# The decay multiplies of a gated linear attention split between VectorE and GpSimd, with all steps laid out anew

## The chip, the cores and the metric

One core of a Trainium2 chip runs the whole program. Its engines are TensorE (PE; its weight loads are shown apart as PEld), VectorE (DVE), ScalarE (ACT), GpSimd (POOL) and SyncE (SP), which here issues all transfers. The metric is the device time of one execution in microseconds. Three runs of the kernel before gave 840.4, 843.08 and 843.6 us; the median is 843.08.

## What is computed

A gated linear attention over 4 batches, 8 heads, 768 tokens and 48 dimensions, with a complex decay for each token and dimension, and a two-layer MLP behind it:

```python
mag = np.sqrt(a_re * a_re + a_im * a_im)
scale = np.minimum(mag, 0.999) / (mag + 1e-06)
a_re_n, a_im_n = (a_re * scale, a_im * scale)
for t in range(S):
    ar, ai = (a_re_n[:, :, t, :, None], a_im_n[:, :, t, :, None])
    new_re = ar * S_re - ai * S_im
    new_im = ar * S_im + ai * S_re
    kv = np.einsum('bhd,bhe->bhde', k[:, :, t], v[:, :, t])
    S_re, S_im = (new_re + kv, new_im)
    y[:, :, t] = np.einsum('bhd,bhde->bhe', q[:, :, t], S_re)
...
x = np.ascontiguousarray(attn_out.transpose(0, 2, 1, 3)).reshape(B * S, H * D)
h = x @ w_in                                           # 384 -> 2048
g = np.maximum(h, 0.0) + alpha * np.minimum(h, 0.0)
return (g @ w_out).astype(np.float32)                  # 2048 -> 384
```

All of it is in float32; the weights arrive as 64-bit floats and are turned into float32 on the chip.

## The kernel before

The sequence is cut into 24 units of 128 tokens (4 batches of 6). The recurrence inside a unit isn't run token by token: a unit's queries and keys are multiplied by products of decays level by level, with block lengths h = 1, 2, 4, 8, 16, 32. At level h each block of 2h tokens has a left and a right half; keys of the left half meet queries of the right half in small TensorE products (`ps_lv`, L678), these are masked into the tiles `A` (L699 on ACT, L702 on DVE), and all of them multiply the values (`ps_y`, L817). Then the level's halves are multiplied with their decays, so that the next level can use them. What a unit leaves to later ones goes through the state `St` (L826, L829, and `ps_kv`, L797), and its part of the output through L841; L855 copies the output out, and it goes to DRAM and comes back as `xT` for the MLP.

`KQ` holds a unit's queries and keys: 96 partitions (48 dimensions, real and imaginary), and on each partition queries or keys x 8 heads x 128 tokens. `T` holds the tree of decay products. L661 and L663 turn queries and keys by their phases `PP`. The six levels are done in three visits of two levels, `VISITS = [(1, 2), (4, 8), (16, 32)]`. In each visit ACT copies the operands that TensorE needs gathered (`WQ`, L740: queries and keys of a level; `W`, L756: keys alone), DVE does the first level's multiply, then TensorE does both levels' products (`meet`), then DVE does the second level's multiply. That multiply is `step` (L717): one DVE operation on 1024 elements of each of the 96 partitions, 512 of queries (right halves) and 512 of keys (left halves). The transposed keys (`ps_kt`, L785) come behind the last level.

The decay products themselves (`gates`) are computed for half a batch at a time: ACT and DVE do the large operations (L253 to L318, L338, L426, L429), POOL the small ones for all batches but the first (L318 to L411: chains of small multiplies that depend on each other). POOL also does one step of the weights' conversion (L515, 16 times); DVE does the steps behind it (L517, L519).

The MLP runs for groups of one or two units as soon as their `xT` is there: 672 products for the hidden features (`ps_h`, L889, three for each of 16 feature blocks), ACT and DVE evict them through the activation (L896, L898) into `g_sb`, and 384 products give the output (`ps_o`, L908). Two `ps_h` buffers and one `ps_o` buffer are used in turn.

What sets the order: every part of the work is a Python generator that yields before each operation, and `ORDER` is a long string in which each letter says which generator goes on next (A to I the nine gate groups, J the loads of queries, keys, phases and decays, K and L the values, M pieces of the weights, N and O their conversion, P to m the 24 units, n the loads of `xT`, o the MLP). The arguments of a `yield` (an engine, a size, what it waits for) are not used at run time here: `DVE = ACT = POOL = PE = DMA = step` with a `step` that returns nothing. So each engine's instruction stream is fixed by the string, each engine runs its stream in order, and semaphores hold an instruction until its inputs are written and its buffers are free. `KQ` has three buffers, `T` two, `WQ` two, `W` one, `PP` one.

Of the kernel before, what the change touches and what calls it, by code (L numbers as in the profile page):

```python
# [14 lines left out]
ALU = mybir.AluOpType  # L15
# [15 lines left out]
    "AAAAAAAAAAAAAAAABJJJJBBAAAAAAAAMMMMMAMAAAAAAAAAAALLLBBNNBBLABLAAALABALAAAANBNABBBBANAABABBANABOOAMBB"  # L31
    "OBBOAAAAAAKMAABBBABABABABABBAKKKKAALLKAABABABAABAABNAAAAABANBABALAAABAABNBNOBBBBOOOOBONBMNBNNBBBBNNJ"
    "OBOOOOOBBPBPCBNPCBBBBPCBBBBCCJJJOBBOBBKPPPPBCBBBBBMPNJJLNNBPNNBPBPBPBCNPBNCMBMCPPPPPJPCKKKKKKKKKKKKK"
    "BKBKPBBBMBCPBNOCNBOOBPCMNCLLCCBLPPPPPPPPPPPPPPPPCCMCBCCBKCCCPJOCOCDOJOCNNJCNNNNNCDCCKKKPCPCPPPPPPPPP"
    "CCQCOKOOOCMQCCQLDDDQCCLLLLLLJLLLLLLCLCCCJDJJJJJJJCCNJQQCDNCQCQCDDQQCDCCNNQCDDQQDDQCOCODDCDCDCCCQDDOQ"
    "CQOCQQQCDDDDKOCRQQCRQQQQQQCQQQRRRRQQQQQMnQCNDMCOCOOCDDDMCQCLQCLRCCCCRCRRLLLRCRRRoKJLQOOOOCoRoCoCRRCR"
    "oQQLLLLLoooKLLQLoQQQoQCoCDCooRooQoRRDooCCCCRRRRRRRRRRoCRCoCoCoCDoRQCJJJEooRRODooooNNNNNoEDRooRoRoooo"
    "RDnLLLLooOoOoOoRODLooRoLLLLLLRLLDNRNoLSoooooooooSoRRRRRooJJSooOoooooSoSSDSNDSSSESoooooooRoSNSSoooSDo"
    "ooSSSDJSJJEJJJJJJDoooooDoooEOSSSSooooSDoooSSSSSSooDDDDDDDooETTSSSEESooooSSSSSToSSEEESSooKSSSoSToJTTT"
    "ToooToooSToooTooSLoooToULoDLLoLDTJDDDDDDJTDoToEDTDDoDLDLoDDDDDDooLLLLLoToTLTooooooooooToTTTUTTToTooT"  # L40
    "ooTLJooDTTToooDUUTTTTTToULLLLULEEEEooEoTEoEDDDDDDDDDoDDEooooooUEToooUUUoooooonoUoEooJoUoooooUEUEDTDD"
    "DoTTUUUELEJULoooLLKLLLLKoUoooooDDooDDDJoKDKKoKoooUUUUUUooooDDDTTTTTToUoooUDUUUooooUooDUEDUUUUEUEEEoo"
    "EoEoooooooEoEEUooUooJooEoooUUUUoUUoFUUoooEEEoEoEooooooooooEEoEoEVFooFoJVVooJoFoJJnooooJJJJVJVFoLLooo"
    "oooooVVVFFLoLVoooooooooEEEEEEVoooVVVEEEEEEEEEEELEEEoEJJJooFoWWoEEoEEEVooooVVooVoooWJVVVVFLoooWooLooo"
    "oWVVVVVVWVWWJVoooVFFVooooXVWLoLLLVLLoLooKVKoEEEEWEVVVVVVVVVVVKLLWEEVoKooLLLLLooLXFWLVLLVLVLVVWWWWWoE"
    "EEEELooWooooEoEoEWEEEooJEWWWWWWWWEoooooooooJJEoEJEEEoooEWWWooooWoooWWWWWWWWWXLoooooWoFFFLXoLLXXXoXXo"
    "GLLWWooJoJLLXooXoXWWWWWWooooFoFFXXXXXXFoLooooLooFoXoFoFFFFFFFJJooFooonXoXXXXXGLLLLooFFXooooooXXXXooo"
    "XoXoFYFFFooooFoooFooXoFXXXXXXXXXFFXXXXXJJoYYJoooooLJLJFFFGoooFYLGFFFFFFFFooXoooYYYYYJYoYooXoooooooLo"
    "FFFFFoZZYYYYJooJYoYYZooooooYoooooZGoYYYYYYYYoYFLZZZZZZZFooooLoYYLFFLGFLLLLFLLooooYYoZZoYYYJYYYYJJLJJ"
    "LLGoFZZZLLFLLFLLLLFLooooLFFFFFFFFFFFooZZYooFFFFYZoGGGGFoooFYYYYYYYYZZZoooFooLooooFFFFFFZJFFFZooZZZZZ"  # L50
    "FZFoooooJZooZoZZnZZZZooZZZZZJZaZZLLFFJoLooooZZZJoooFoGaooGooaoaooooGGGLLLLLLLoLLLaaaaoooooooooaJaJaJ"
    "ooooooaGaaaaaoooHoooHoaaooooooGGoooaaGaaaGGaaaGGGooGGGooboaaaKboooooJooooooaooooaHGbGaGJGbJoaaGaabbb"
    "bJoJaaaaaabaaGLLbLLLoGoLGoLLLGaaHooHJooobboGoooooobboooGHobbbHobbooooJbooGHoJoboLHGJoooGbbbGbGbbbbJb"
    "ooocooooGoooJoonbooKoKGccoKKKKKooooooLbcccGcccooooHoooocooGoLLLbGJoJobbbobHbHGHHbbbLbHbGbbbbbLbbboGG"
    "GGGHoHoHoLoooGGGGGoGcGLcoGoGooGGGoGoGoGcGcGcccccLJoJoLooLoooLooooLLLcccLLccLdocoJocGcoGcGccGoocodooc"
    "oHHHddcHcccccccHdLcGGcGKoooLLHHGGHLoHLJLLHHoHooHooHooHdcGcdcdddcHcccooodoooGoooGGGGoGLLdLLLLLoGGGodd"
    "dddoooododoooonooooGooGodGddddooGdoddoooooooGHGddHoodJodHHHoJoJJJHHHJJJooooodooooooddddddddddddddddo"
    "HJeeooooJooooeoooooeoHooHHHHHHHdoLeeeooooooeeeeoefoofoooeeeoeoeooooJJooofLoooooLLooIeeofffeJeeooKooo"
    "oLLLLLLLLLHeeeeeeeeHHHHLooHoHoHoHeHoHeHooeeeeeeeeeeeeeeeJJIJJLLoHHeeHooHHIHfKHHfHHHHHoooHoJHoHooHffJ"
    "ooHoofgIooogoooofffILoHHoofffHoofofHHogHooooLnooooLLLooLoJoLgLHKLffffffffggoLIILggggfoooofKooooKHooL"  # L60
    "HooHgHooooHoHKKoKKHoofoIfKooofffoffffffffffLfJoJoofHfffHoooooHggggggoLLLLLooooIogoogIoooooHggIIIIooo"
    "ooooLgoggLgLLLILoooogggggoooIgILoooogggggggggggggJJJoohJJhhoLLIIJoooJJoggLgoooJooohhILLLoIoInoooLoho"
    "oiiJJhJohoLLJLLLhooooIIooooooooohhohhoIooooooihIhhhoIhhhoIIoIoIhIIIooiooooooooIIIihihhhhhhhooohLILIo"
    "oIooooIohooJJhJooohohoohhhhhIIIiIhIhhLhhhhLLoLooooiiiiooLoooLooooiiiooihohihhihooioioooooooJijJjiiJJ"
    "JIIIIIIIIIIIIIIIIIIIIIIIIIIooiooooIojooiooioioioooooiooooIIijIIIoIIoojjjjjILoIiiIoILoLILoLoLLLiijiij"
    "ioiLLLLLLLjjjLLLiLLoooIIIIIoooiooIIIIIiooooooooooooooijjjojojooLLoooooooojjjjijjjjIIiiiiooojoojooiii"
    "jjjIooJjjjjjjjjjjjjnjoJJJjjjjooooooooooooookooookokokooLoooLJJJJJJJooooooLookkooookkokokookookooookk"
    "kkkkkLLLooooooLLLLLLLoooookkkkoookkkkokooLookookkllokokkJkkkkkkkkkkkkkkololooooooooLLoooLooookLooLLL"
    "LllllllllLoLoooooooooJooooooooooooooooooooooonooooooooooooooooooJoooLLLollloooooooolllloooJooooooJJl"
    "loooooJLlllllllllooooooooololoolllllllllllllllllooooooomooooLoooomoooooooooomooooommmmmmomooooomoooo"  # L70
    "ooooLmmLmLLoooonooLomooooooooomLmmmLooooLLommmmmmmmoooooooomomomLLooooooooooomoooooooLomommmmmmmmmmm"
    "mmmomooooooooooooooooooooooooooooooooooooooooooooooooooooooooooooooooonooooooooooooooooooooooooooooo"
    "oooooooooooooooooooooooooooooooooooooooooooooooooooooooooooooooooooooooooooooooooooooooooooo")
# [28 lines left out]
def kernel(  # L102
# [542 lines left out]
    def unit(u):  # L645
# [62 lines left out]
        def step(h, x0=None):  # L708

            at = TL - TL // h if h > 1 else 0  # L710
            if h > 1:
                x, m = ([(2 * h, H * P // (2 * h)), (H * P - h, 2), (1, h)], [(TL, H), (1, P // h), (0, h)])
            else:
                x, m = ([(H * P - 1, 2), (P, H), (2, HC)], [(1, 2), (TL, H), (2, HC)])
            x = bass.AP(tensor=KQ.tensor, offset=KQ.offset + h, ap=[KQ.ap[0]] + x)
            m = bass.AP(tensor=T.tensor, offset=T.offset + at, ap=[[T.ap[0][0], D2]] + m)
            nc.vector.tensor_tensor(out=x, in0=x if x0 is None else x0, in1=m, op=ALU.mult)  # L717

        if c == 0:
# [4 lines left out]
            k_ = yield DVE(H * D, k_, ("start", 0))  # L724
            nc.vector.tensor_tensor(out=St, in0=St, in1=start[:, b].unsqueeze(2).to_broadcast([D2, H, D]), op=ALU.mult)
            state[b] = (St, k_)
        k_ = r
        for visit in VISITS:
            ready = []
            for h in visit:  # L730
# [270 lines left out]
```

## Time and profile before

| What | Value |
| --- | --- |
| median of three runs | 843.08 us |
| the profiled execution | span 845.2 us |
| PE busy | 699.6 us (83% of the span) |
| DVE busy | 653.3 us (77%), 1020 instructions |
| ACT busy | 443.3 us (52%) |
| POOL busy | 196.3 us (23%), 293 instructions |
| DMA queue q1 | 129.20 MB, 59.2% of 16 engines |
| L717, the decay multiplies | 144 on DVE, 178.7 us busy |
| feature and output products, L889 and L908 | 302.0 and 295.2 us busy |

The span is cut into 40 equal slices; each digit is the busy share of an engine in tenths:

```profile
PE   0002316688899999999999999999999999999998
DVE  5999998689998999979998997687877656345212
ACT  7679686356745656665565634555444324233211
POOL 6241421126544411450115404300124000000000
```

Busy time counts from an instruction's start to its end, also where it stands still in between because of something else. Neighbouring instructions of one engine overlap by some 0.08 us. The chain that ended last (each step followed back to what released it) is 63% PE and 17% DVE.

### The profile page before, as it was taken

The page shows a single profiled execution, that of the slowest core. Times are in us where ns is not written, and L with a number is a line of the kernel's source. Part 1 is how long each engine was busy: PE and PEld are TensorE (multiplying, and loading weights), DVE is VectorE, ACT ScalarE, POOL GpSimd, SP SyncE. Part 2 cuts the span into 40 slices and gives each one's busy share as a digit, 9 for nine tenths or more (in the row PEclk, how much of TensorE's full clock was granted, in tenths as well). Part 3 has the DMA queues.
Part 4 walks back from the last instruction along what each step waited for, and adds up shares of the span by engine and source line. Part 5 has one row for each costly group of instructions (what it writes and reads, how often), then busy time and mean ns, then how long its engine had stood idle before and what let it go on. Part 6 is the DMA issues. An engine that isn't in the chain of part 4 may idle for free.

```text
span 845.2 us, 26866 instructions
## 1 busy us (share of the span) xinstructions
PE 699.6 (83%) x11488; PEld 529.6 (63%) x11488; DVE 653.3 (77%) x1020; ACT 443.3 (52%) x937; POOL 196.3 (23%) x293
## 2 busy tenths in 40 slices
PE   0002316688899999999999999999999999999998
PEld 0001315566777777767777777777676777777776
DVE  5999998689998999979998997687877656345212
ACT  7679686356745656665565634555444324233211
POOL 6241421126544411450115404300124000000000
PEclk9999997879999999999999999999999999999999
DMA  8496987675469677736965467747644482231100
GB/s 240 142 270 172 281 198 207 186 203 123 118 201 255 143 182 223 182 88 172 264 166 138 134 178 181 201 107 192 159 136 106 115 204 64 69 80 38 37 29 9
DMA packets 194174, 130.91 MB, mean 155 GB/s; under 512 B 74120, under 2 KB 185864, under 8 KB 194056
## 3 DMA queue, kind: packets, MB, share of 16 engines
q1 hardware_dynamic: 194056, 129.20, 59.2%
q8 instruction: 90, 1.47, 0.8%
q14 instruction: 28, 0.23, 0.1%
HBM read 100.82 MB, written 35.71 MB: 162 GB/s over the span
## 4 chain that ended last, share of the span: by engine, by line
PE 63%; DVE 17%; DMA 6%; issue 6%; ACT 5%; SPq 2%; POOL 0%; DVEq 0%; ACTq 0%; POOLq 0%
PE ps_o L908 25%; PE ps_h L889 25%; PE ps_lv L678 4%; DVE KQ L717 4%; PE ps_y L817 3%; PE ps_kv L797 2%; PE ps_y L841 2%; DVE gate L338 2%; DMA PP<-phs 2%; DMA phs<-gate 1%; DMA g_sb<-in_w_in_dram 1%; PE ps_kt L785 1%; DVE gate L426 1%; SPq L626 1%; DVE gate L340 1%
## 5 line engine op out<-in xcount | busy, mean ns | idle before, releaser
L889 PE MATMUL ps_h<-xT,w_in_sb 128*128 128x256 f32 (+1 forms) x1344 | 302.0, 356 | 2.9 <-DVE g_sb L898 1.6
L908 PE MATMUL ps_o<-w_out_sb,g_sb 128*128 128x384 f32 x768 | 295.2, 499 | 5.1 <-DVE g_sb L898 4.9
L889 PEld LDWEIGHTS ps_h<-xT,w_in_sb 128*128 128x128 f32 x1344 | 234.3, 193 | 74.1 <-issue 3.6
L898 DVE SCALAR_TENSOR_TENSOR g_sb<-g_sb,al,ps_h 128x256 f32<-128x256 f32 (+1 forms) x224 | 97.4, 437 | 115.5 <-ACT g_sb L896 115.1
L896 ACT ACTIVATE g_sb<-ps_h 128x256 f32<-128x256 f32 (+1 forms) x224 | 79.0, 353 | 204.2 <-PE ps_h L889 202.7
L908 PEld LDWEIGHTS ps_o<-w_out_sb,g_sb 128*128 128x128 f32 x768 | 138.0, 192 | 56.7 <-DVE g_sb L898 6.9
L717 DVE TENSOR_TENSOR KQ<-KQ,T 96x1024 f32<-96x1024 f32 x120 | 148.5, 1239 | 32.1 <-PE ps_lv L678 23.2
L678 PE MATMUL ps_lv<-WQ 96*32 96x32 f32 x2304 | 34.7, 204 | 79.0 <-DVE WQ L661 55.9
L678 PEld LDWEIGHTS ps_lv<-WQ 96*32 96x32 f32 x2304 | 26.6, 116 | 99.7 <-DVE WQ L661 56.1
L740 ACT COPY WQ<-KQ 96x1024 f32<-96x1024 f32 x48 | 50.0, 1041 | 27.8 <-DVE KQ L717 27.7
L338 POOL TENSOR_TENSOR gate<-gate 128x72 f32<-128x72 f32 x42 | 29.6, 704 | 125.6 <-ACT gate L368 122.8
L855 ACT COPY T<-ps_y 48x256 f32<-48x256 f32 x96 | 30.8, 364 | 51.8 <-PE ps_y L841 51.2
L338 DVE TENSOR_TENSOR gate<-gate 128x576 f32<-128x576 f32 (+5 forms) x84 | 50.0, 595 | 1.1
L515 POOL TENSOR_SCALAR top<-top 128x768 f32<-128x768 f32 x16 | 41.5, 2602 | 32.1 <-ACT top L507 32.1
L678 PE MATMUL ps_lv<-KQ,W 96*32 96x32 f32 x1536 | 25.2, 205 | 27.5 <-ACT W L756 23.2
L817 PE MATMUL ps_y<-A,VL 64*48 64x64 f32 x2304 | 42.4, 223 | 4.1 <-DMA VL<-vsc 2.5
L699 ACT ACTIVATE A<-ps_lv,columns 128x64 f32<-128x64 f32 x144 | 36.2, 336 | 17.2 <-PE ps_lv L678 17.1
L426 DVE TENSOR_TENSOR gate<-gate 128x1152 f32<-128x1152 f32 (+2 forms) x36 | 43.6, 1235 | 0.3
L756 ACT COPY W<-KQ 96x512 f32<-96x512 f32 x48 | 30.8, 642 | 23.9 <-DVE KQ L717 21.1
L817 PEld LDWEIGHTS ps_y<-A,VL 64*48 64x48 f32 x2304 | 39.8, 124 | 5.5 <-DMA VL<-vsc 2.7
L678 PEld LDWEIGHTS ps_lv<-KQ,W 96*32 96x32 f32 x1536 | 20.3, 115 | 29.6 <-ACT W L756 24.7
L785 PE MATMUL ps_kt<-ident,KQ 96*128 96x96 f32 x192 | 26.0, 260 | 15.4 <-DVE KQ L717 12.9
(106 smaller groups left out, 912.1 us busy)
## 6 DMA issues: line engine op xcount, KB each, us to landing
T<-decs SPq DMA_DIRECT2D x48, 384.0 KB
PP<-phs SPq DMA_DIRECT2D x24, 387.0 KB
KQ<-in_q_dram SPq DMA_DIRECT2D x48, 192.0 KB
decs<-gate SPq DMA_DIRECT2D x7, 1152.0 KB
phs<-gate SPq DMA_DIRECT2D x14, 576.0 KB
KQ<-in_k_dram SPq DMA_DIRECT2D x40, 192.0 KB
vsc<-in_v_dram SPq DMA_DIRECT2D x48, 144.0 KB
VL<-vsc SPq DMA_DIRECT2D x24, 288.0 KB
```

The source lines that it names most:

```text
L338: on(4 * k).tensor_tensor(out=m, in0=w[:, 1::-1].unsqueeze(2).to_broadcast([P, 2, 2, k]), in1=pairs_of(u), op=ALU.mult)
L426: TT(out=m[:, a], in0=U5[:, 1 + a], in1=turned(off3, o)[:, a].unsqueeze(1).unsqueeze(3).to_broadcast([P, L // 2, nb, 2]), op=ALU.mult)
L515: nc.gpsimd.tensor_scalar(out=top, in0=top, scalar1=F64_SMALL, scalar2=None, op0=ALU.max)
L678: nc.tensor.matmul(t[64 * i + j:64 * i + j + HC // 2, p], lhsT=keys(n, g), rhs=queries(n, g), start=True, stop=True)
L699: nc.scalar.activation(a[:, :, cols], t[:, :, at:at + name], AF.Copy, scale=s)
L717: nc.vector.tensor_tensor(out=x, in0=x if x0 is None else x0, in1=m, op=ALU.mult)
L740: nc.scalar.copy(z.rearrange("p i n t -> p i (n t)").rearrange("p i (m h) -> p m i h", h=h), bass.AP(tensor=KQ.tensor, offset=KQ.offset + ...
L817: nc.tensor.matmul(o, lhsT=Vp[h][64 * i:64 * i + 64, s, e_ * D:(e_ + 1) * D], rhs=a, start=False, stop=False)
L889: nc.tensor.matmul(p, lhsT=w_in_sb[:, f // 2, kk, f % 2 * P:(f % 2 + 1) * P], rhs=x_of[m][:, kk], start=(kk == 0), stop=(kk == NK - 1))
L896: nc.scalar.activation(gt, p, AF.Relu, scale=-1.0)
L898: nc.vector.scalar_tensor_tensor(out=gt, in0=gt, scalar=al_1[:, f:f + 1], in1=p, op0=ALU.mult, op1=ALU.add)
L908: nc.tensor.matmul(sums[0], lhsT=gt[:, c * P:(c + 1) * P], rhs=w_out_sb[:, f], start=(f == 0), stop=(f == NF - 1))
```

## The change

`step` no longer does queries and keys in one DVE operation. It is a generator with an index i (0 for the queries, 1 for the keys): the keys' 512 elements go to GpSimd, the queries' 512 to VectorE. Queries and keys have each their own chain of steps (`kq` and `kk`), and the keys' step is issued first. The elements written are the same as before. `ORDER` is replaced by a new string of 4436 letters (4292 before; the 144 more are the second operation of each step).

```diff
 ORDER = (
-    "AAAAAAAAAAAAAAAABJJJJBBAAAAAAAAMMMMMAMAAAAAAAAAAALLLBBNNBBLABLAAALABALAAAANBNABBBBANAABABBANABOOAMBB"
...
+    "AABAMAAAAAAAAAAMMMAAAAAAAAAAAANBKNKJMMAKJAAAAAAAAAAAAAAAAABANAJAAKAKAABAJAAAAAAKABAAMBKAAAAAAAAAAAAA"
...
-        def step(h, x0=None):
+        def step(h, i, *after):
 
             at = TL - TL // h if h > 1 else 0
-            if h > 1:
-                x, m = ([(2 * h, H * P // (2 * h)), (H * P - h, 2), (1, h)], [(TL, H), (1, P // h), (0, h)])
-            else:
-                x, m = ([(H * P - 1, 2), (P, H), (2, HC)], [(1, 2), (TL, H), (2, HC)])
-            x = bass.AP(tensor=KQ.tensor, offset=KQ.offset + h, ap=[KQ.ap[0]] + x)
-            m = bass.AP(tensor=T.tensor, offset=T.offset + at, ap=[[T.ap[0][0], D2]] + m)
-            nc.vector.tensor_tensor(out=x, in0=x if x0 is None else x0, in1=m, op=ALU.mult)
+            m = [(P, H), (2 * h, P // (2 * h)), (1, h)]
+            x = bass.AP(tensor=KQ.tensor, offset=KQ.offset + (H * P if i else h), ap=[KQ.ap[0]] + m)
+            e = yield (POOL if i else DVE)(H * HC, *after, *[("decays", u)] * (h == 1))
+            T = L["T"]
+            d = bass.AP(tensor=T.tensor, offset=T.offset + at + i, ap=[[T.ap[0][0], D2], (TL, H), (2, P // (2 * h)), (0, h)])
+            x0 = WQ[:, i].unsqueeze(3) if h == 1 else x
+            (nc.gpsimd if i else nc.vector).tensor_tensor(out=x, in0=x0, in1=d, op=ALU.mult)
+            return e
...
-                    w = yield ACT(2 * H * HC, k_, takes=(R[held],))
+                    w = yield ACT(2 * H * HC, kq, kk, takes=(R[held],))
...
-                        w = yield ACT(H * HC, k_, takes=(R[held],))
+                        w = yield ACT(H * HC, kk, takes=(R[held],))
...
-                    k_ = yield DVE(2 * H * HC, w, *[("decays", u)] * (h == 1))
-                    T = L["T"]
-                    step(h, WQ if h == 1 else None)
+                    kk = yield from step(h, 1, kk, w)
+                    kq = yield from step(h, 0, kq, w)
...
-            if visit[-1] != 1:
-                k_ = yield DVE(2 * H * HC, e)
-                step(visit[-1])
+            kk = yield from step(visit[-1], 1, e)
+            kq = yield from step(visit[-1], 0, e)
...
-            e = yield PE(0.333, k_, takes=(R["misc"],), n=2)
+            e = yield PE(0.333, kk, takes=(R["misc"],), n=2)
...
-            e = yield PE(0.47, q_, known, mode=1, n=8)
+            e = yield PE(0.47, kq, known, mode=1, n=8)
```

The new string gives every engine's stream a new order: PE, DVE, ACT and SP keep their counts of instructions (the 144 multiplies stay on DVE, half as long), POOL gets 144 more. The lines of the changed kernel stand one to three lines lower than those of the kernel before (L719 is its `step`).

## The prediction

> **What bounds the kernel now.** I read the busy times by stage first, because the share over the whole span mixes a start, a middle and a tail. The columns are the window, then the busy us of PE, PE's weight loads, DVE, ACT and POOL (number of instructions in brackets), the granted clock, the DMA share and GB/s.
>
> ```profile
> 0.00:100.00 100.00, 13.93 (x428) 11.44 (x428) 87.37 (x194) 77.30 (x113) 39.12 (x44) 1.00 0.79 213
> 100.00:200.00 100.00, 57.88 (x1190) 45.04 (x1190) 87.06 (x149) 61.40 (x112) 17.44 (x15) 0.88 0.74 200
> 200.00:300.00 100.00, 96.22 (x1768) 74.99 (x1768) 93.46 (x133) 59.68 (x136) 54.48 (x72) 1.00 0.68 167
> 400.00:500.00 100.00, 99.00 (x1580) 73.47 (x1579) 91.68 (x126) 57.50 (x123) 25.74 (x42) 1.00 0.66 171
> 600.00:700.00 100.00, 96.39 (x1539) 71.90 (x1537) 73.09 (x107) 38.07 (x99) 18.31 (x38) 1.00 0.54 135
> sum 845.20, PE 699.59 PEld 529.56 DVE 653.35 ACT 443.34 POOL 196.27; mean PE 87.45 PEld 66.20 DVE 81.67 ACT 55.42 POOL 24.53
> ```
>
> PE has 700 us of work in a span of 845 us and stands idle 142 us in gaps between matmuls, nearly all of it before 200 us. After that it is full; its matmul stream is fixed in order, so whatever makes PE wait again is added to the end. DVE is the second full engine: about 90% until 500 us, then 75%. So until about 500 us two engines run full side by side, and the written order decides how well they mesh. A DVE relief can gain only by filling PE's idle start, and a DVE that comes later than its order expects costs PE time.
>
> Next come the groups by form (line, engine, operation, tiles, shape, count, then busy us and mean ns of one):
>
> ```profile
> L717 DVE TENSOR_TENSOR KQ<-KQ,T 96x1024 f32<-96x1024 f32 x120 | 148.5, 1239 | 32.1 <-PE ps_lv L678 23.2 <-ACT WQ L740 7.9
> L826 DVE TENSOR_TENSOR St<-St,T 96x384 f32<-96x384 f32 x44 | 26.7, 606 | 0.4
> L396 POOL TENSOR_TENSOR gate<-gate,runs 128x252 f32<-128x252 f32 x12 | 10.1, 842 | 29.6 <-ACT runs L368 21.2 <-ACT gate L391 7.9
> L411 POOL TENSOR_TENSOR gate<-gate 128x288 f32<-128x288 f32 x6 | 5.8, 975 | 0.5
> ```
>
> Then the two engines' timelines in one place (start us, us, engine, line). DVE first, POOL second:
>
> ```profile
> 547.17 1.22 DVE L717 TENSOR_TENSOR KQ<-KQ,T 96x1024 f32<-96x1024 f32 x1
> 548.31 1.82 DVE L717 TENSOR_TENSOR KQ<-WQ,T 96x1024 f32<-96x1024 f32 x1
> 550.05 0.47 DVE L898 SCALAR_TENSOR_TENSOR g_sb<-g_sb,al,ps_h 128x256 f32<-128x256 f32 x1
> ```
>
> ```profile
> 547.25 1.80 POOL L411 TENSOR_TENSOR gate<-gate 128x288 f32<-128x288 f32 x1
> ```
>
> The two hold each other up. POOL's multiply takes 0.79 us when undisturbed (the least of its six) and takes 1.80 here, because a DVE multiply already runs until 548.39; DVE's next multiply, normally 1.22 us, takes 1.82: it gets going only at about 548.9, when POOL is nearly through at 549.05. The DVE instruction held up has two inputs in SBUF. The eviction L898, with one input in PSUM, takes 0.47 us beside POOL as without it, as does L702 (0.41 us). The same is seen early, beside POOL's L515:
>
> ```profile
> 44.75 2.54 POOL L515 TENSOR_SCALAR top<-top 128x768 f32<-128x768 f32 x1 [6.68 <-ACT top L507]
> ```
>
> ```profile
> 45.22 0.83 DVE L338 TENSOR_TENSOR gate<-gate 128x48 f32<-128x48 f32 x1
> 46.08 0.18 DVE L340 TENSOR_TENSOR gate<-gate 128x24 f32<-128x24 f32 x1
> 46.30 0.21 DVE L338 TENSOR_TENSOR gate<-gate 128x48 f32<-128x48 f32 x1
> ```
>
> The first L338 takes 0.83 instead of 0.21 us, the ones behind it run free while POOL still counts as busy. So POOL shuts out DVE for only a part of its instruction: 0.63 us of L515, 0.60 us of L411.
>
> **The change part by part.** *What DVE saves.* The 144 multiplies (24 units, six levels) go from 1024 to 512 elements. Undisturbed, 1024 elements take 1.22 us and 384 elements (L826, most of its instances) 0.55, so 512 take 0.55 + 128 x 0.67/640 = 0.68. Saving 0.54 each, 77 us in all, of DVE's 653.
>
> *What POOL gets.* 144 multiplies of 96x512 with two inputs. The trace has none so long. Undisturbed instances of POOL's two-input multiplies: 72 elements 0.31 us, 252 elements 0.68, 288 elements 0.79; that is 2.1 ns an element, so 512 take 0.79 + 224 x 0.0021 = 1.27 us. The bounds are the means of the disturbed rows, scaled alike (0.975 + 0.47 = 1.45), and 1.2. In all 183 us on top of POOL's 196: POOL isn't full anywhere (57 us of the first 200, plus 38 for five units there).
>
> *What the shutting out costs DVE.* L411 (288 elements) holds 0.60 of 0.79 us; 0.19 us of it, start and end, holds nothing. So 512 elements hold 1.27 - 0.19 = 1.08 us: twice what DVE saves. It depends on how often DVE has a two-input multiply to start at that time. Share f of the hold that DVE lost: L515 in the first 140 us, sixteen times, 7.9 of 10.2 us, 0.77; L411, 2.5 of 3.6 us, 0.71; L396 and L399, the shorter multiplies, about 0.3. The new hold is longer than any, which argues for the high end; DVE idles 10% of this stage and a quarter of its work reads PSUM, which argues against. I take f = 0.55 and keep 0.3 and 0.75. Per step DVE loses 1.08 x 0.55 = 0.59 and saves 0.54: the relief is gone.
>
> [...]
>
> *What the new order makes of it.* PE's stream is rewritten. I counted, in both programs' instruction order, the MLP matmuls ahead of the end of each unit, and DVE's work up to each unit's sixth multiply with the durations of the rows above. Unit 12 (the thirteenth) decides. Before: its sixth multiply starts at 436.05 us, DVE's listed durations up to there add to 432, its last PE matmul ends at 454; 291 feature matmuls and 144 output matmuls stand ahead. After: DVE's durations add to 392, 40 less, and 278 and 134 stand ahead, which at 0.43 and 0.66 us each (six matmul records of L889 take 1.29 us in the chain, four of L908 1.32) is 12 us less PE work. So the new order counts on this unit some 12 us and more earlier, less of the matmul stream is there to cover it, and DVE has 78 x 0.59 = 46 us of new holds against its 40: it comes 6 us later than before. PE's idle time grows by 6 + 12 = 18 us.
>
> The same reckoning elsewhere: unit 4, DVE 5 us less, 30 holds 18 us, and 15 us more MLP ahead: -2. Unit 9, 32 less, 36 of holds, 8 less MLP: +12. Unit 16, 50 less, 61 of holds, 10 less MLP: +21, but DVE has free time there. So the damage is done between units 5 and 13, and 18 us stands for it: 845.2 + 18 = 863. The profiled execution lies 2.1 us above the median of the runs, so 861 in the terms of the runs. With f = 0.3 unit 12 gives 25 - 40 + 12 = -3 (840); with f = 0.75, 63 - 40 + 12 = +35 (878).
>
> *Moved at no price:* ACT's copies and SP's transfers are the same in number, in a new order. DVE and PE wait 11.5 us in all for DMAs, so that order is worth between -12 and +12; I take 0. The first multiply of a unit waits for the same T and PP; a second wait in front of an operation is one more semaphore instruction (21 ns at L717, median), 0.02 us a level, and hidden while DVE is full.
>
> **The rivals.** *(a) The keys' half comes late.* Before, both halves of a level are ready 1.22 us after its start. Now the keys' half takes 1.27 plus POOL's wait: its instructions lost 87 us on 293 to waits by their undisturbed times, 0.3 us each, so +0.35 us a level. Behind it wait ACT's copies WQ and W (in order, with the MLP's evictions behind them), PE's meetings and the transposes; POOL's own gate chains and weights lie behind steps that wait. Uncovered that is 6 x 0.38 = 2.3 us a unit, 55 us in 24 units. For it: ACT W and WQ waited 49 us for L717 already. Against: DVE, not the chain, is late. Half uncovered: 863 + 27 = 890, 888 in the runs' terms.
>
> *(b) The relief holds; faster.* Holds fall into DVE's gaps and its PSUM work. With f = 0 no unit is later than its place in PE's stream: unit 5 has 8 us less DVE work but 8 us more MLP ahead, so PE can start its MLP earlier by 16 us at most: 845 - 16 = 829, 827 in the runs' terms. For it: f was 0.3 for the shorter multiplies, and over all POOL instructions 14 of some 36 us. It decides below f = 0.33 (40 - 12 = 28 of 84 us).
>
> *(c) It comes out even,* f near 0.33: 843, give or take 4.
>
> **How the numbers follow.** The forecast has 0.48, (a) 0.20, (b) 0.22, (c) 0.10. A measurement can tell 0.5%, about 4 us, from no change. Faster 0.22, same 0.10, slower 0.68. The range for 8 in 10 leaves out the far end of (b) and of (a): 830 to 893; the forecast's own range is 847 to 878.
>
> **What would show it.** In the changed profile: POOL's 96x512 multiplies at 1.27 us at best and well above in the mean; DVE's 96x512 near 0.7 us with a tail to 1.7; DVE's busy time not 77 us lower but within 30 us of 653, since a DVE instruction held up counts as busy; the gate multiplies (L338, L426) and L661 longer in the mean; PE idle in the stretch 200 to 500 us, where it had 7 us. I am wrong if DVE's busy time falls under 600 us and PE is full from 190 us on; and if PE's gaps are ended by ACT W and WQ behind POOL while DVE has time to spare, it is (a).

## The result and the profile after

The changed kernel takes 930.6 us (median of four runs, 928.8 to 933.4), the kernel before 842.2 us beside it (840.4 to 843.6). The ratio is 1.107, with a 95% interval of 1.103 to 1.111: 88 us slower. The forecast was 861 us with a range of 830 to 893. The direction was right; the size was missed by 70 us, beyond the range.

The profiled execution has a span of 931.7 us (845.2 before). PE is busy for 722.7 us (699.6), DVE for 656.7 us (653.3), ACT for 439.2 us (443.3) and POOL for 407.5 us (196.3). The granted clock is 0.935 in the mean (0.986). The span in 40 equal slices, from the page of the changed kernel; each digit is a busy share in tenths, and the last line is the granted clock:

```profile
PE   0000425788798898898988899999999999999998
DVE  5999998798897789688966966876767454353112
ACT  6756656566445553474554425742343342233221
POOL 5324443457945753575258515843472132031000
PEclk9999756899999899899999989999999999999999
```

Before, PE reached the 9s in its twelfth slice and stayed there. Now it moves between 7 and 9 until the 23rd, in slices of 23.3 us (21.1 before). POOL, mostly at 0 to 5 in the middle before, is mostly at 3 to 7. The clock falls as low as 5 in the start. The chain that ended last was 63% PE and 17% DVE before; on this page it is

```profile
PE 45%; DVE 24%; POOL 9%; DMA 7%; issue 7%; ACT 5%; SPq 3%; DVEq 0%; POOLq 0%; ACTq 0%
```

so a larger part of the end is set by the work of other engines, VectorE's (24 instead of 17%) and GpSimd's (9 instead of 0%). By stages (window, then busy us of PE, weight loads, DVE, ACT and POOL with instructions, clock, DMA share, GB/s):

```profile
0.00:100.00 100.00, 8.63 (x302) 7.33 (x306) 85.29 (x182) 67.38 (x100) 40.73 (x48) 1.00 0.73 204
100.00:200.00 100.00, 52.26 (x1145) 42.26 (x1138) 89.35 (x139) 60.22 (x104) 45.52 (x29) 0.69 0.61 170
200.00:300.00 100.00, 84.19 (x1428) 65.14 (x1427) 86.28 (x127) 54.20 (x122) 62.10 (x65) 0.95 0.67 170
...
400.00:500.00 100.00, 87.44 (x1517) 64.43 (x1516) 79.51 (x107) 54.13 (x120) 59.27 (x71) 0.97 0.58 157
...
600.00:700.00 100.00, 94.68 (x1459) 70.64 (x1458) 69.83 (x101) 39.00 (x99) 50.11 (x63) 0.98 0.55 143
...
sum 931.70, PE 722.72 PEld 544.95 DVE 656.66 ACT 439.23 POOL 407.52; mean PE 72.27 PEld 54.49 DVE 65.67 ACT 43.92 POOL 40.75
```

The trace's first record of the granted clock is at 101 us, so the 1.00 of the first window measures nothing. Two things stand out beside the same windows of before. From 200 to 500 us PE had 96 to 99 us in each 100; now it has 84 to 87. And DVE, which held 92 to 93 us there, is not busier there but less busy: 79 to 86. So neither engine is full in the middle. Over the whole span PE stands idle 205 us (142 before), of which 139 (128) lie before 200 us, and its 11,488 instructions take 23 us more at the lower clock. 63 and 23 make the 86 us between the two spans.

The groups by form (line, engine, operation, tiles, shape, count, then busy us and mean ns of one, then idle time before them):

```profile
L719 POOL TENSOR_TENSOR KQ<-KQ,T 96x512 f32<-96x512 f32 x120 | 179.8, 1501 | 210.7 <-ACT WQ L743 124.3 <-ACT W L759 40.8 <-PE ps_lv L680 35.6
...
L719 DVE TENSOR_TENSOR KQ<-KQ,T 96x512 f32<-96x512 f32 x120 | 106.6, 891 | 35.8 <-PE ps_lv L680 23.2 <-ACT WQ L743 12.5
...
L398 POOL TENSOR_TENSOR gate<-gate,runs 128x252 f32<-128x252 f32 x12 | 17.4, 1448 | 3.8 <-ACT runs L370 3.3
...
L342 DVE TENSOR_TENSOR gate<-gate 128x288 f32<-128x288 f32 x49 | 29.6, 604 | 1.1
...
L827 DVE TENSOR_TENSOR St<-St,T 96x384 f32<-96x384 f32 x44 | 31.6, 719 | 0.4
```

One of these groups in the kernel before, where it is L340:

```profile
L340 DVE TENSOR_TENSOR gate<-gate 128x288 f32<-128x288 f32 x49 | 23.4, 478 | 0.7
```

And the shortest, median and longest duration (ns) of the multiplies that start a unit, from the view of one line's instructions:

```profile
L719 POOL TENSOR_TENSOR KQ<-WQ,T x24: 1277/1296/1824, 55.2 to 830.1; 96x512 f32<-96x512 f32 x24
L719 DVE TENSOR_TENSOR KQ<-WQ,T x24: 677/690/1790, 59.5 to 830.7; 96x512 f32<-96x512 f32 x24
```

At the start of a unit GpSimd's half takes 1.28 to 1.30 us undisturbed and VectorE's 0.68 to 0.69; at later levels GpSimd's shortest is 1.05 us. In the mean GpSimd's takes 1.44 to 1.50 us, VectorE's 0.89. The gate multiplies of L342 (L340 before) went from 478 to 604 ns and L827 (L826 before) from 606 to 719 ns, and GpSimd's own gate multiplies of L398 (L396) from 842 to 1448 ns, though nothing was changed in them. The timelines of one place show why (start us, us, engine, line). VectorE's:

```profile
296.78 2.00 DVE L665 TENSOR_TENSOR KQ<-KQ,PP 96x1024 f32<-96x1024 f32 x1
298.70 0.68 DVE L719 TENSOR_TENSOR KQ<-KQ,T 96x512 f32<-96x512 f32 x1
```

GpSimd's in the same place:

```profile
296.60 1.10 POOL L719 TENSOR_TENSOR KQ<-KQ,T 96x512 f32<-96x512 f32 x1
298.86 1.68 POOL L719 TENSOR_TENSOR KQ<-WQ,T 96x512 f32<-96x512 f32 x1 [1.16 <-DMA vsc<-in_v_dram]
```

L665 takes 1.22 us when nothing disturbs it. It takes 2.00 us here, since GpSimd's multiply began 0.18 us before it. The next GpSimd multiply in turn meets a VectorE multiply already running and takes 1.68 instead of 1.28 us. Summed over the trace, DVE's instructions lose 89 us to this (14 us before), worked out as each duration less the undisturbed one of its form.

### The profile page after: what moved, and what is told of

Read it like the earlier page. It is cut to its first block, busy times and chain, and to the rows that moved or that the text cites. A ratio compares the mean times of both kernels' runs of the same rounds, so it can differ in the third digit from the quotient of the medians.

```text
span 931.7 us, 27129 instructions
## 1 busy us (share of the span) xinstructions
PE 722.7 (78%) x11488; PEld 544.9 (58%) x11488; DVE 656.7 (70%) x1020; ACT 439.2 (47%) x937; POOL 407.5 (44%) x437
## 3 DMA queue, kind: packets, MB, share of 16 engines
q8 instruction: 91, 1.49, 0.7%
## 4 chain that ended last, share of the span: by engine, by line
PE 45%; DVE 24%; POOL 9%; DMA 7%; issue 7%; ACT 5%; SPq 3%; DVEq 0%; POOLq 0%; ACTq 0%
PE ps_o L909 18%; PE ps_h L890 17%; DVE gate L340 3%; DMA T<-decs 3%; DVE KQ L719 3%; PE ps_lv L680 3%; POOL KQ L719 3%; PE ps_y L818 2%; DVE gate L342 2%; DVE gate L428 2%; PE ps_kv L798 2%; PE ps_y L842 2%; DVE g_sb L899 1%; POOL gate L340 1%; DVE top L519 1%
## 5 line engine op out<-in xcount | busy, mean ns | idle before, releaser
L909 PE MATMUL ps_o<-w_out_sb,g_sb 128*128 128x384 f32 x768 | 309.5, 519 | 21.3 <-DVE g_sb L899 15.9
L890 PE MATMUL ps_h<-xT,w_in_sb 128*128 128x256 f32 (+1 forms) x1344 | 308.7, 365 | 9.7 <-DVE g_sb L899 9.6
L890 PEld LDWEIGHTS ps_h<-xT,w_in_sb 128*128 128x128 f32 x1344 | 243.1, 200 | 90.3 <-DVE g_sb L899 15.4
L719 POOL TENSOR_TENSOR KQ<-KQ,T 96x512 f32<-96x512 f32 x120 | 179.8, 1501 | 210.7 <-ACT WQ L743 124.3
L909 PEld LDWEIGHTS ps_o<-w_out_sb,g_sb 128*128 128x128 f32 x768 | 143.1, 199 | 78.1 <-DVE g_sb L899 18.2
L719 DVE TENSOR_TENSOR KQ<-KQ,T 96x512 f32<-96x512 f32 x120 | 106.6, 891 | 35.8 <-PE ps_lv L680 23.2
L680 PE MATMUL ps_lv<-WQ 96*32 96x32 f32 x2304 | 34.8, 204 | 83.4 <-DVE WQ L663 51.1
L719 POOL TENSOR_TENSOR KQ<-WQ,T 96x512 f32<-96x512 f32 x24 | 34.6, 1443 | 135.8 <-DVE KQ L665 56.0
L680 PEld LDWEIGHTS ps_lv<-WQ 96*32 96x32 f32 x2304 | 27.0, 116 | 99.7 <-DVE WQ L663 51.1
L818 PE MATMUL ps_y<-A,VL 64*48 64x64 f32 x2304 | 43.4, 223 | 19.6 <-issue 19.3
L340 DVE TENSOR_TENSOR gate<-gate 128x576 f32<-128x576 f32 (+5 forms) x84 | 54.0, 643 | 1.8 <-ACT gate L370 0.5
L680 PE MATMUL ps_lv<-KQ,W 96*32 96x32 f32 x1536 | 25.5, 206 | 36.9 <-ACT W L759 15.1
L818 PEld LDWEIGHTS ps_y<-A,VL 64*48 64x48 f32 x2304 | 40.6, 125 | 21.2 <-issue 20.5
L428 DVE TENSOR_TENSOR gate<-gate 128x1152 f32<-128x1152 f32 (+2 forms) x36 | 45.8, 1298 | 0.1
L680 PEld LDWEIGHTS ps_lv<-KQ,W 96*32 96x32 f32 x1536 | 20.7, 117 | 38.9 <-ACT W L759 20.7
L701 ACT ACTIVATE A<-ps_lv,columns 128x64 f32<-128x64 f32 x144 | 37.4, 337 | 12.3 <-PE ps_lv L680 12.3
```

Of the source, the lines that this page charges most:

```text
L340: on(4 * k).tensor_tensor(out=m, in0=w[:, 1::-1].unsqueeze(2).to_broadcast([P, 2, 2, k]), in1=pairs_of(u), op=ALU.mult)
L428: TT(out=m[:, a], in0=U5[:, 1 + a], in1=turned(off3, o)[:, a].unsqueeze(1).unsqueeze(3).to_broadcast([P, L // 2, nb, 2]), op=ALU.mult)
L680: nc.tensor.matmul(t[64 * i + j:64 * i + j + HC // 2, p], lhsT=keys(n, g), rhs=queries(n, g), start=True, stop=True)
L701: nc.scalar.activation(a[:, :, cols], t[:, :, at:at + name], AF.Copy, scale=s)
L719: (nc.gpsimd if i else nc.vector).tensor_tensor(out=x, in0=x0, in1=d, op=ALU.mult)
L818: nc.tensor.matmul(o, lhsT=Vp[h][64 * i:64 * i + 64, s, e_ * D:(e_ + 1) * D], rhs=a, start=False, stop=False)
```

## The experiments

All kernels of this section but o_broken330 (ten times) were run once, beside the kernel before at 842.0 to 844.5 us. Since repeated runs of the kernel before lay between 840 and 849 us, differences under some 5 us between single runs are not read.

**Is it the order or the split?** Four kernels take the change apart: the new order with the keys' multiplies left out (so VectorE keeps its whole relief and GpSimd does nothing new); the new order with one whole multiply on VectorE; and the old order with the split, and with the keys' multiplies left out.

n_no_keys, against the changed kernel:

```diff
-            (nc.gpsimd if i else nc.vector).tensor_tensor(out=x, in0=x0, in1=d, op=ALU.mult)
+            if not i:
+                nc.vector.tensor_tensor(out=x, in0=x0, in1=d, op=ALU.mult)
```

> The new order, the keys' multiplies left out altogether (the queries' half stays on DVE), so the output lacks the keys' decays. Exclusion theory (DVE and POOL shut each other out, DVE stands 89 us longer in its instructions, POOL 135): with the holds gone the new order works as laid out, 820 to 850 us, DVE busy about 580. Latency theory (the keys' 1.27 us on POOL is too long for the chain of a level): the same here. Order theory (the new order is bad by itself): still over 890 us.

n_whole_dve, against the changed kernel:

```diff
-            (nc.gpsimd if i else nc.vector).tensor_tensor(out=x, in0=x0, in1=d, op=ALU.mult)
+            if i:
+                return e
...
+            nc.vector.tensor_tensor(out=x, in0=WQ if h == 1 else x, in1=m, op=ALU.mult)
```

> The new order, but each level's multiply as one operation of 1024 elements on DVE, at the queries' place, nothing on POOL. Exclusion theory: no holds beyond the 14 us of the kernel before, but DVE has the 77 us more that the new order does not count on: 850 to 885 us. Latency theory: the chain has its 1.22 us again, 845 to 870. Order theory: 900 us or more.

o_split, against the kernel before (o_no_keys is the same with `((0, nc.vector),)` as the list):

```diff
-            nc.vector.tensor_tensor(out=x, in0=x if x0 is None else x0, in1=m, op=ALU.mult)
+            m = [(P, H), (2 * h, P // (2 * h)), (1, h)]
+            for i, engine in ((1, nc.gpsimd), (0, nc.vector)):
...
+                engine.tensor_tensor(out=x, in0=x if x0 is None else x0[:, i].unsqueeze(3), in1=d, op=ALU.mult)
```

> The old order, each level's multiply split as in the change (keys on POOL, queries on DVE, both issued where the one stood). Exclusion theory: the holds come with the split whatever the order, DVE's saving of 77 us is eaten, and the chain of a level is longer: 880 to 930 us. Latency theory: the same, 880 to 920. Order theory: within 15 us of the kernel before, 830 to 860.

> The old order, the keys' multiplies left out, nothing on POOL in their place (the output lacks the keys' decays). It is what DVE's relief of 77 us is worth when it costs nothing. If DVE's time set the pace of the old order: 800 to 825 us. If the fixed order of PE and the chains set it: 835 to 845.

Measured, in us:

| | old order | new order |
| --- | --- | --- |
| one multiply on VectorE | 843 | 910 (n_whole_dve) |
| split | 924 (o_split) | 931 |
| keys' multiplies left out | 857 (o_no_keys) | 877 (n_no_keys) |

Two expectations were missed, and the misses say most. First, o_no_keys takes 74 us of work off VectorE, adds nothing anywhere, and is not faster but slower, 857 us. Its windows:

```profile
200.00:300.00 100.00, 97.42 (x1635) 75.78 (x1636) 79.94 (x130) 57.24 (x135) 32.90 (x67) 0.97 0.68 168
...
400.00:500.00 100.00, 97.09 (x1567) 72.36 (x1567) 78.23 (x122) 55.85 (x121) 19.53 (x42) 0.98 0.63 167
```

VectorE fell from 92 or 93 to 78 or 80 us in each 100, and PE had been full there already; in the first 200 us PE has 72.1 us of work done, against 71.8 before. So in this order the start is not set by VectorE's amount of work, and the relief had nothing to fill. The granted clock here is 0.97 to 0.98, where the kernel before had 1.00, and the same matmuls take longer (PE 705.5 us instead of 699.6). What else makes this kernel slower than the one before was not tried. Second, the new order without any new GpSimd work fell between the two expected bands: 877 us. The new order and the split both cost, and they don't add: the split costs 80 us in the old order and 21 in the new one, the order 66 us with a whole multiply and 7 with the split. The new order counts on VectorE's relief (910 without it, 877 with it), the old one has no use for it.

**Where does the split cost?** The old order, with the split in units 0 to 13 only, where VectorE is full, and in units 14 to 23 only:

```diff
+            if u < 14:
+                m = [(P, H), (2 * h, P // (2 * h)), (1, h)]
+                for i, engine in ((1, nc.gpsimd), (0, nc.vector)):
...
+                return
```

> The old order, the split for units 0 to 13 alone (the stretch to about 500 us, where DVE was 90% busy), the old multiply for the other ten. The whole split cost 79 us in this order. If it costs where DVE is full, as I forecast: nearly all of it, 905 to 925. If every unit pays alike: 14/24 of it, 885 to 895.

> The old order, the split for units 14 to 23 alone (from about 500 us on, where DVE had a quarter of its time to spare). If it costs where DVE is full: 843 to 852. If every unit pays alike: 10/24 of 79 us, 870 to 882.

Early 910 us, beside 843.8: 66 us, or 4.7 a unit. Late 859 us: 15 us, or 1.5 a unit. The two add up to the whole split's 80. The cost is three times as dense where VectorE is full, but the late units are not free, so the second expectation hit neither band.

**Shut-out, lateness or GpSimd's queue?** The split does three things at once. GpSimd's multiply shuts VectorE out (the 89 us lost above, against 14 before); the keys' half arrives later; and GpSimd's share of the gate work stands in its in-order queue behind multiplies that wait (in the changed kernel GpSimd idles 210.7 us just before the 120 multiplies of L719's first row). First, lateness and queue without the shut-out: memsets, which read nothing, in place of GpSimd's multiply (two of them 1.09 us, three 1.63 us).

```diff
-            (nc.gpsimd if i else nc.vector).tensor_tensor(out=x, in0=x0, in1=d, op=ALU.mult)
+            if i:
+                for _ in range(BLIND):
+                    nc.gpsimd.memset(x, 0.0)
```

> The new order; in place of each keys' multiply POOL writes zeros over the same elements, twice in a row: it keeps POOL and the chain waiting for something near the multiply's time, but reads nothing from SBUF. The output lacks the keys. Exclusion theory: DVE's instructions lose almost nothing, and the time is within 15 us of the run without keys. Latency theory: the chain is as long as in the changed kernel, so over 890 us. Order theory: over 890 us.

> The new order with POOL writing zeros over the keys three times in a row instead of multiplying: about 1.6 us a step, as long as the multiplies take in the changed kernel with their waits (1.49 us in the mean), but without reading SBUF (the output lacks the keys). If the exclusion costs by holding DVE up: within 12 us of the run with two (884 us), 880 to 896. If it costs by making the keys' half late on the chain: 905 to 930.

> The old order with three memsets of GpSimd (some 1.63 us together) over the keys' half in place of its multiply: late on the chain but without a read, so that VectorE's instructions should show some 15 us of excess only. The keys' half is zeroed at each step. If lateness is the loss, 905 to 930 us; if the shut-out is, 860 to 880 us (the new order lost 19 us by the same edit, 896 against 877).

884 us with two, 896 with three (at the edge of the band for no shut-out) and, in the old order, 900 us, between its bands. In all three VectorE's instructions lose 14 to 15 us, as in the kernel before: the memsets leave it alone, so what these runs lose is lateness and queue.

Then the shut-out and the queue with the keys' half off the chain: GpSimd does a multiply of 96x512 from the gathered copies of the keys (`WQ` and `W`; `KQ` itself at the last level) into a part of T that nobody reads any more.

```diff
-            (nc.gpsimd if i else nc.vector).tensor_tensor(out=x, in0=x0, in1=d, op=ALU.mult)
+            if not i:
+                nc.vector.tensor_tensor(out=x, in0=x0, in1=d, op=ALU.mult)
...
+                idle = T[0:D2, :, 0:HC].rearrange("p n (m h) -> p n m h", h=h)
+                nc.gpsimd.tensor_tensor(out=idle, in0=seen, in1=d, op=ALU.mult)
```

> The new order with the keys' half taken off the chain: GpSimd still does a multiply of 96x512 per step from the same sources, but writes it to a part of T that nobody reads, so no step waits for it (the keys then go on undecayed). Against the 877 us without the keys' multiplies: if the rest of the loss is the time that GpSimd's multiply shuts VectorE out, it is all here, 905 to 930 us with some 75 us of excess in VectorE's instructions; if it is the keys' half coming late, 877 to 890 us, with the same excess. Between them, the time divides the loss.

> The same in the old order: GpSimd's multiply of 96x512 into a part of T that nobody reads, the queries' half on VectorE, the keys undecayed. Against the 857 us of the old order without the keys' multiplies and the 924 us of the old order with the split: shut-out alone 900 to 925 us; lateness alone 857 to 870 us.

929 us in the new order, 897 in the old one, 3 below its upper band. Something is still late in them: ACT waits until GpSimd is through with `W` and `T`, 10.8 us in all in o_hold and 5.3 in n_hold. And last the queue alone, where these waits are 2.7 and 2.1 us:

```diff
-                nc.gpsimd.tensor_tensor(out=idle, in0=seen, in1=d, op=ALU.mult)
+                nc.gpsimd.tensor_tensor(out=idle[:, 0, 0:1], in0=seen[:, 0, 0:1], in1=d[:, 0, 0:1], op=ALU.mult)
+                for _ in range(2):
+                    nc.gpsimd.memset(idle, 0.0)
```

> The old order as in o_hold, but in GpSimd's queue one multiply of a few elements per step (it waits for the same data) and two memsets of 96x512 behind it, all to the part of T that nobody reads: GpSimd's queue stands as long as in o_hold (some 1.25 us a step), with no shut-out and nothing late but GpSimd's own gate work. The keys go on undecayed. If o_hold's 897 us are the shut-out, 857 to 870 us here; if they are GpSimd's gate work late behind the multiplies, 885 to 900 us.

> The same in the new order, beside n_hold's 929 us and 877 us without the keys' multiplies. Shut-out: 877 to 892 us; GpSimd's queue: 910 to 930 us. n_blind3, which also had the queue, gave 896, so 877 to 895 is expected.

874 us in the old order, a little above its band for the shut-out, and 904 in the new one, in neither band: 9 us above what was expected, and 8 above n_blind3. GpSimd's busy time is much the same with and without the shut-out (382 us in n_queue, 396 in n_hold), and the groups show what differs. n_hold's:

```profile
L720 DVE TENSOR_TENSOR KQ<-KQ,T 96x512 f32<-96x512 f32 x120 | 103.0, 860 | 43.5 <-PE ps_lv L680 25.8 <-ACT WQ L755 17.6
...
L342 DVE TENSOR_TENSOR gate<-gate 128x288 f32<-128x288 f32 x49 | 31.5, 643 | 1.1
```

n_queue's:

```profile
L720 DVE TENSOR_TENSOR KQ<-KQ,T 96x512 f32<-96x512 f32 x120 | 85.2, 712 | 54.1 <-PE ps_lv L680 37.4 <-ACT WQ L757 16.6
...
L342 DVE TENSOR_TENSOR gate<-gate 128x288 f32<-128x288 f32 x49 | 23.0, 469 | 1.1
```

All of VectorE's instructions together lose 80 us in n_hold and 13 us in n_queue. As a ladder, each step adding mainly one thing:

| | old order | step | new order | step |
| --- | --- | --- | --- | --- |
| keys' multiplies left out | 857 | | 877 | |
| and GpSimd's queue stands (queue) | 874 | +17 | 904 | +27 |
| and VectorE is shut out (hold) | 897 | +23 | 929 | +25 |
| and the keys' half is late (the split) | 924 | +26 | 931 | +1 |
| queue and late, no shut-out (blind3) | 900 | | 896 | |

In the old order it closes from the other side too: queue and lateness make 900, and 857 + 17 + 26 is 900. There all three causes weigh about alike, with up to 8 us of the shut-out's 23 in ACT's waits for `W` and `T`. In the new order the late half costs nothing that shows, but the other two are not cleanly parted. Queue and lateness without the shut-out cost 7 us with two memsets (n_blind), 19 with three and 27 in n_queue, which leaves 25 to 47 us for the shut-out (929 less 904, 931 less 896, 931 less 884). That n_queue takes longer than n_blind3, which has the queue and lateness besides, is not explained; in the traces PE waits 31 us for VectorE in n_queue and 20 in n_blind3 (the 51 us before its first matmul aside). A part of most steps is PE's own instructions at a lower granted clock: PE is busy for 705.5, 706.4, 712.9 and 723.7 us down the old order's column (mean clock 0.976, 0.978, 0.973 and 0.936) and for 703.2, 715.6, 716.9 and 722.7 us down the new one's (0.979, 0.948, 0.941 and 0.935). How a queue that stands costs time is seen in what ACT waits for in o_queue (us in total, times, longest):

```profile
ACT runs L366 <- POOL gate L340: 20.0, 5, 8.3
...
ACT gate L413 <- POOL gate L411: 7.6, 6, 2.1
```

Neither wait is among those of o_no_keys at more than 1.1 us. ACT's gate step stands behind GpSimd's, and ACT also evicts the MLP's products.

Does it matter which half is late? The halves exchanged in the new order:

```diff
-            (nc.gpsimd if i else nc.vector).tensor_tensor(out=x, in0=x0, in1=d, op=ALU.mult)
+            (nc.vector if i else nc.gpsimd).tensor_tensor(out=x, in0=x0, in1=d, op=ALU.mult)
```

> The new order with the halves exchanged: the queries' half on GpSimd and the keys' on VectorE, the same work, the same shut-out. If the loss hangs on the keys' half being late in particular, 900 to 920 us; if on the shut-out, or on any half being late, 922 to 940 us.

938 us: not faster, so the loss doesn't hang on the keys' half in particular.

**What makes the new order slow by itself?** In the changed kernel PE waits for "issue", which is time in which it waits for nothing that the profile shows (us in total, times, longest):

```profile
PE ps_y L818 <- issue: 19.3, 9, 4.9
PE ps_lv L680 <- issue: 19.1, 9, 7.1
...
PE ps_y L842 <- issue: 4.5, 4, 1.8
```

and in the kernel before:

```profile
PE ps_lv L678 <- issue: 5.6, 3, 2.2
...
PE ps_y L808 <- issue: 2.2, 1, 2.2
```

All such rows together are 45.6 us after, in 23 waits, and 12.3 before, in 8. The page lists a DMA queue of the kind "instruction", q8, with 91 packets and 1.49 MB in 932 us, that is blocks of 16 KB. Of the 23 waits 22 (38 us) end between 1.2 and 1.7 us after a block has landed, and so do all 8 of the kernel before and all 25 of n_no_keys. With a block every 10 us, chance would put about one in twenty there, so these are read here as PE waiting for its next instructions. (The other one, 7.1 us long, ends 20 us after a block and is something else.) PE has the most instructions for its time in the short products of the attention, four for each product (two matmuls, two weight loads): 2304 matmuls of L818 keep it busy for 43.4 us, 768 of L909 for 309.5. A block of instructions would be used up fastest there, an estimate from these rows. The start aside, the new order has 19 runs of more than 448 PE instructions without an MLP matmul between them, 14 of them of 520, while the old one has four, all of 456. So three kernels draw MLP steps into the long runs (runs over 400 with and without the keys' multiplies, and over 260), and one does so in the kernel before (runs over 330). Each moves letters of the order only; where runs over 400 are broken, one moved MLP step then reads weights ahead of their conversion. The first of the changed strings in n_broken (the rest left out):

```diff
-    "CKCRQCRCCQLQLRLQRMQQQQLoCCRORRoQORCRRDCMRoQMCCCCQQCRCQCCQQQQDQQRCROOCQCCODNOQOOQOOORoDooooQRRLLoRRQL"
+    "CKCRQCRCCQLQLRLQRMQQQQLoCCRORRoQORCRRDCMRoQMCCCCQQCRCQCCQQQQDQQRCoooROOCQCCODNOQOOQOOORDooQRRLLoRRQL"
```

> The new order without the keys' multiplies (as in the run of 877 us), with one change: where over 400 PE instructions of the attention would stand in a row, the next MLP matmul is drawn forward into them (36 letters move; no run is longer than 400 after the start). Code theory: PE runs out of instructions in long rows of short matmuls; the 44 us of PE's waits that nothing in the profile ends fall to some 15, the time to 845 to 860 us. If the rows are not the cause of these waits: they stay at 35 to 45 us and the time at 870 to 885. The output lacks the keys' decays.

> The changed kernel, with its order altered in the same 36 places. Code theory: PE's waits that nothing ends fall from 46 to 15-20 us and the time from 931 to 900-912 us. Otherwise 925 to 935.

> The changed kernel with MLP matmuls drawn forward wherever over 260 PE instructions of the attention would stand in a row (60 letters move; none is drawn past the weights' conversion or a load of xT). Code theory: PE's waits that nothing ends fall from 46 to 10-25 us, the time from 931 to 895-915 us. Otherwise 920 to 935.

> The kernel before, with MLP matmuls drawn forward wherever over 330 PE instructions of the attention would stand in a row (26 letters move). Its waits that nothing ends are 12 us. Code theory: some 6 to 8 of these go, 0.990 to 0.995 of the time before. Otherwise 0.998 to 1.005.

Without the keys' multiplies 868 instead of 877 us; with the split 924 (over 400) and 924 (over 260) instead of 931; in the kernel before 844.3 against 843.8 us, a ratio of 0.9998 (95% interval 0.9971 to 1.0025). So breaking gains some 7 to 9 us where the runs are long, less than the code theory said, and nothing where they are short. With the split, PE's waits that nothing ends fall from 46 to 32 us (over 400) and 30 us (over 260), not to the 10 to 25 us of the theory. The waits of PE behind the first pair, n_no_keys:

```profile
PE ps_y L819 <- issue: 22.4, 12, 3.2
...
PE ps_y L843 <- issue: 10.2, 7, 2.3
...
PE ps_lv L680 <- issue: 8.1, 5, 2.4
```

and n_no_keys_broken:

```profile
PE ps_y L819 <- issue: 14.2, 9, 3.1
...
PE ps_lv L680 <- issue: 7.3, 6, 1.8
...
PE ps_y L843 <- issue: 4.8, 6, 1.1
```

All "issue" rows of the two are together 44.2 and 30.0 us: 14 us less, beside 9 us less time. The gaps are a real cost of the new order, and long runs are part of what makes them, but breaking the runs removed only a third; the other two thirds stayed.

What the rest of the order's price is made of can be read in n_whole_dve, which does the operations of the kernel before in the new order:

```profile
PE ps_lv L680 <- issue: 13.2, 7, 4.7
PE ps_y L826 <- issue: 9.3, 6, 3.2
...
PE ps_y L850 <- issue: 8.5, 6, 1.8
```

Its span is 63 us longer than the kernel's before (908.0 us). Of these, 21 are such waits (33.7 us in all, against 12.3), 19 are PE's own instructions at a mean clock of 0.945 instead of 0.986 (718.4 us, against 699.6), and 22 are longer waits of PE for other engines, for ACT above all (66 us, against 49). This divides the price, but what in the order makes ACT late was not tried.

## Why the prediction was wrong, step by step

- **What POOL and VectorE's multiplies take: right.** 1.27 us was forecast for GpSimd's half, 1.28 to 1.30 came at the first level (1.05 at the least at others), 1.44 to 1.50 in the mean, at or just over the upper bound of 1.45. VectorE's half was put at 0.68 us and takes 0.67 to 0.69.
- **The shut-out: right.** 0.59 us lost per multiply was forecast; 75 us more lost over 144 multiplies is 0.52, a share f of 0.48 for the assumed 0.55. VectorE's busy time stayed within 4 us of before, as the forecast said it would. 
- **"What the new order makes of it": this step failed, in what it gave the order and the relief.** Without any hold (f = 0, rival (b)) the forecast has the new order at 827 us, 16 us faster than before. n_no_keys, in which nothing new on GpSimd holds VectorE up, takes 877 us and is 33 us slower. That is 50 of the 70 us missed. For the order itself the forecast had a term of 12 us ("12 us less PE work" ahead of unit 12); with the old operations in it the order costs 66 us (n_whole_dve, 910 against 844), and with the relieved work still 20 us (877 against 857). In n_whole_dve the sixth multiply starts 12 us later than before in unit 0, 17 in unit 4, 33 in unit 12 and 62 in unit 20. In the changed kernel it is 15, 31, 47 (483.5 us instead of 436.1) and 84 us. So the loss grows by some 3 us a unit from the first on and is not made between units 5 and 13; for unit 4 the forecast had -2.
- **The holds in the same step came nearer, and the balance was wrong in kind.** From f = 0 to f = 0.55 the forecast's time rises by 34 us (827 to 861); from n_no_keys to the changed kernel it rises by 54 (877 to 931), of which 25 to 47 are the shut-out and the rest mostly GpSimd's queue. The forecast set 40 us saved on VectorE against 46 us lost as if both reached the end in full. The runs hand on only a part: 67 us more lost to the shut-out (80 in n_hold, 13 in n_queue) cost 25 us, 76 us less to do from n_whole_dve to n_no_keys bring 33 us, and in the old order 74 us less to do bring nothing (857 against 843).
- **The reading behind it: "two engines run full side by side".** VectorE was 90% busy but in the old order not a second bound. With 78 to 80% of it in use, o_no_keys had PE just as full. What the order needs is each result at its place in the in-order queues. In the changed kernel VectorE idles more while it does the same work; its wait for ACT's eviction, before and after:

```profile
DVE g_sb L898 <- ACT g_sb L896: 115.1, 95, 3.9
```

```profile
DVE g_sb L899 <- ACT g_sb L897: 183.8, 115, 5.2
```

- **Put at nothing: waits for instructions and GpSimd's queue.** That PE would run short of instructions (12 us before, 38 after) was not among the steps. GpSimd's queue, 17 us in the old order and 7 to 27 in the new one (the lower figures with the late half), was noted under rival (a) ("POOL's own gate chains and weights lie behind steps that wait") and priced at nothing of its own.
- **Moved at no price:** PE and VectorE wait for DMAs 14 us in all (11.5 before), so the order of the transfers was indeed worth little by these waits. GpSimd's waits for DMAs (83 us at its multiplies, 32.5 of them in one wait for T) are not in this sum; what they cost was not tried.
- **The rivals.** (a), the late keys' half, was put at 55 us uncovered. It is 26 us in the old order and about 1 in the new one: the new order covers it, and only (a)'s remark on the queue bore out. Its own sum slipped too, from 0.35 us a level to 0.38. (b), the relief holds, is ruled out: with no keys' multiplies at all, and so with f = 0, the new order takes 877 us and not 827. (c), even, likewise.
- **The test it named.** PE idle between 200 and 500 us: from 7 us to 41 us, as it said. Its sign for (a), PE's gaps ended by ACT's `W` and `WQ`, did not come: 43 us of such waits, against 45 before.
- **The clock.** 23 of the 86 us of span are PE's own instructions taking longer at 0.935 instead of 0.986, with 0.69 between 100 and 200 us (0.88 before). How far the gaps cause it was not tried. In the changed kernel's trace the granted clock is 0.50 from 105 to 149 us, where PE stands still five times for 3.9 to 7.3 us; 32 matmuls of L680 take 0.65 to 0.66 us in this stretch, and 0.46 and 0.49 us right behind it, where the clock is 1.00.

## What to carry to other kernels

In an order written out by hand for in-order engines, time saved on an engine that is not the bound has no price until a kernel with that work left out shows one: the same relief of some 75 us brought nothing in the old order and 33 us in the new. Measure a new order by itself first, with the old operations in it: here it cost 66 us before the split cost anything. When work moves to an idle engine, price three things apart: what it shuts out, what comes later, and what already stood in that engine's queue (23, 26 and 17 us here in the old order).

## What the runs showed of the hardware

- GpSimd's memsets of 96x512 (0.52 to 0.55 us each) left VectorE alone, which lost 13 to 15 us over the whole kernel, as without them (14); its multiply of the same size, with two inputs, made that 80 to 89 us.
- In the changed kernel, with 11,488 matmul records and as many weight loads, 22 waits of PE, 38 us, ended 1.2 to 1.7 us after a block of 16 KB had landed on the queue of the kind "instruction".
- The granted clock differs between kernels with the same matmuls on one core: 0.986 in the kernel before, 0.98 in both kernels without the keys' multiplies, 0.935 in the changed one.
